# A linear-attention block gated by a spatial-shift MLP: the same instructions in another planned order

## The chip, the cores and the metric

One core of a Trainium2 chip. The time is the device time of one execution in microseconds (us); "before" is the median of three executions. Five engines run instruction queues of their own, each strictly in order: PE (matrix), DVE (vector), ACT (activation), POOL (GpSimd) and SP, which here only issues DMA transfers. They meet through semaphores.

## The reference

With x of 2048 rows and 512 columns, xn its layer norm, and 1376 hidden columns:

```python
phi = lambda t: jnp.where(t > 0, t + 1, jnp.exp(t)) + 1e-6        # 32 heads of 16
num = phi(q) @ (phi(k).T @ v); den = phi(q) . sum(phi(k)) + 1e-6  # per head; q, k, v = xn @ wqkv
s   = (num / den) @ wo
h   = gelu(layernorm(xn) @ w1)          # its four quarters of columns are shifted by
x1  = xn + shifted(h) @ w2              # +1, -1, +2, -2 rows before w2
y   = x1 + gelu(layernorm(x1) @ w3) @ w4
out = x + s * silu(y)
```

All in float32.

## The kernel before

**Tiles.** Rows are taken in 16 tiles of 128 (index i, 0 to 15) and in four blocks of 512 (index b, 0 to 3). Each factor of a product is split into a high and a low part (names ending in h and l), and three matmuls, high by high, low by high and high by low, make one product (`products`, L455). Some products of two-by-two blocks go through `seven` (L749), which makes seven products of 256 columns in three PSUM banks pa, pb and pe; ACT copies finished sums out as p1 and p5 (both shown as p, or pm and the like, in the profile), after which the bank is used again.

**Stages.** First the projections: k (`key`), q (`query`), and `gram`, which adds up k^T xn in four banks g; wq and w1 first have their column means removed (`center`, L546). For wq the four tiles are added on DVE into wqt; for w1 four transfers add them up in the tile w1t, the first by SP and then three accumulating ones by POOL (`gather`); in both cases a matmul (wqm, w1m) makes the column sums from the total. Beside that run the mixer's first product (`mix1`, tiles h and ht), its block forms (`forms`, names hs and ha) and second product (`mix2`, tiles o), then the k-v matrices, then the mixer's two large products (`up_pair`, `down`) with the attention's output (`attend_pair`) between, and the gate and the store (`gate`).

**Scales.** A layer norm takes DVE's bn_stats and bn_aggr (tiles st and mv; L567) and a chain of four small instructions on POOL: add epsilon (w), power of -0.5 (rs, L572), and two small ones for the shift (ns and nm in `scale_x`, L577; nm twice for the second norm). ACT then scales the tile: x for the first norm, y for the second. `scale_u` (L588) makes the per-row factors au of block b in the same way (pu, then power), and `spread_a` (L595) has PE transpose them (bank ab), so that a row of DRAM can be read back by `join_a` (L604) to all partitions as abc.

**Order.** No instruction is issued as the code comes to it. Every one is recorded in a `Plan` (L85) with an engine, a modelled time busy, a modelled latency, its predecessors, and for a transfer its size in MB (`mb`). `deadlines` (L237) gives each PE instruction a nominal time, one after another, and `backward` (L258) gives everything else a due time: that of its successors, less a gap and its own latency, or, for a transfer, less 4.0 us and 4 us per MB. `nudged` (L231) then takes a table of pairs, number of an instruction and quarters of a microsecond, by which that instruction is due sooner (`SOONER`, L1352). `emit` (L264) walks through modelled time: for each engine it lists what could start, keeps those that start within a slack of the earliest, takes the one that is due first, and issues it to that engine's queue. PE may take an instruction out of its recorded order within `window` us of nominal time, and one that opens a new bank within `ahead`. Buffers come from pools with a set number of slots, and SP's and POOL's transfers each go through eight completion slots of their own, so that a transfer waits for the eighth-last of its kind.

The lines that the prediction names: L164 is ACT's activation, L186, L191 and L196 are the two-input, the one-input and the scalar-and-two-input instruction of DVE (or POOL), L145 the matmul, L202 an SP load, L207 an SP store, L220 POOL's accumulating transfer, L569 and L570 the statistics. pqd is the DRAM copy of phi(q): SP stores one part (qr) and POOL adds another (qe). zacc gathers the sums of phi(k) in the same way.

Of the kernel before, what the change touches and what calls it, by code (L numbers as in the profile page):

```python
# [84 lines left out]
class Plan:  # L85
# [82 lines left out]
    def vec(self, eng, out, reads, emit, pair, scalars=0):  # L168
        views = [v for v in reads if isinstance(v, View) and v.n > 4]
        sb = not any(v.tile.psum for v in views + [out])  # L170
        n = max([v.n for v in views] + [out.n])
        if eng == "POOL":
            lat = (.2 if n <= 8 else .15 + n / (435 if pair else 1000))
            return self.add(eng, lat, lat, reads, [out], emit, two=n > 64)
        if pair or not sb:
            lat = .15 + n / 960 + (.06 if scalars else 0)
        else:
            lat = .16 + n / 1920 + (.1 if scalars else 0)
        lat = max(lat, .2)
        self.add(eng, lat - .08, lat, reads, [out], emit, two=sb and n > 8)  # L180
# [77 lines left out]
    def backward(self):  # L258
        for op in reversed(self.ops):
            if op.eng != "PE":  # L260
                for o in op.post:
                    op.due = min(op.due, o.due - self.GAP - (4.0 + op.mb * 4 if op.mb else op.lat))

    def emit(self, first, lead, reserve, window, ahead, table=()):  # L264
        self.deadlines(first)
        self.nudged(table)
        ops = self.ops
        waiting = {op: len(op.pre) for op in ops}
        avail = {e: [] for e in ("PE", "ACT", "DVE", "POOL", "SP")}
        for op in ops:  # L270
            op.ready = 0.0
            if not waiting[op]:
                avail[op.eng].append(op)
        pe = [op for op in ops if op.eng == "PE"]
        head = 0
        free = {e: 0.0 for e in avail}
        slots = {tag: [0.0] * n for tag, n in self.counts.items()}
        port = dma = 0.0
        table = 0
        done = set()  # L280
        slip = 0.0
        left = len(ops)
        while left:
            while head < len(pe) and pe[head] in done:
                head += 1
            front = pe[head] if head < len(pe) else None
            slip = max(0.0, free["PE"] - front.nom) if front else INF
            best = None
            for e, cands in avail.items():
                picks = []  # L290
                low = INF
                for op in cands:
                    s = max(free[e], op.ready)
                    if op.two and s < port:
                        s = port
                    if op.table is not None and op.table != table:
                        s = max(s, free[e] + 1.28)
                    ok = True
                    fresh = [t for t in op.tiles if t.ap is None]
                    for t in fresh:  # L300
                        if t.tag not in slots:
                            continue
                        q = slots[t.tag]
                        need = sum(1 for u in fresh if u.tag == t.tag)
                        if len(q) < need:
                            ok = False
                            break
                        s = max(s, q[need - 1] + self.GAP)
                        if e == "PE":
                            if op is not front and (len(q) < 2 or op.nom - front.nom > ahead):  # L310
                                ok = False
                                break
                        elif t.tag in lead:
                            n = lead[t.tag] * (1.5 if len(q) > reserve[t.tag] else 1)
                            s = max(s, op.due + slip - n - t.early)
                    if not ok:
                        continue
                    if e == "PE" and op.nom - front.nom > window:
                        continue
                    q = s  # L320
                    if op.table is not None and op.table != table and op.due + slip < s:
                        q = s - 1.28
                    picks.append((q, s, op))
                    low = min(low, q)
                if not picks:
                    continue
                slack = .02 if e == "PE" else 0.08
                s, op = min(((s, op) for q, s, op in picks if q <= low + slack), key=lambda x: (x[1].due, x[1].order))
                if best is None or s < best[0]:
                    best = (s, op)  # L330
            if best is None:
                raise RuntimeError("no operation can go: " + str({t: len(q) for t, q in slots.items()}))
            s, op = best
            e = op.eng
            avail[e].remove(op)
            for t in op.tiles:
                if t.ap is None:
                    if t.tag in slots:
                        slots[t.tag].pop(0)
                    t.ap = self.pools[t.tag].tile([t.rows, t.width], t.dtype, tag=t.tag, name=t.name)  # L340
            op.emit()
            op.at = s
            k = self.COLD if e == "PE" and s < self.COLD_TILL else 1.0
            free[e] = s + op.busy * k
            op.end = s + op.lat * k
            if op.mb:
                soft = e == "POOL"
                late = min(.92, 1.03 * max(0.0, dma - s))
                dma = max(dma, s + (.97 if soft else .06)) + op.mb * (4.59 if soft else 3.43)
                op.end = max(dma + (1.89 if soft else 1.29) + late, s + (4.08 if soft else 2.08 if op.loads else 2.2))  # L350
            if op.two:
                port = op.end if e == "POOL" else free[e]
            if op.table is not None:
                table = op.table
            for t in op.tiles:
                t.left -= 1
                t.end = max(t.end, op.end)
                if not t.left and t.tag in slots:
                    slots[t.tag].append(t.end)
            for o in op.post:  # L360
                flow = o.pre[op]
                if o.eng == e == "PE" and not flow:
                    r = 0.0
                elif o.eng == e:
                    r = op.end
                else:
                    r = op.end + self.GAP
                if op.mb:
                    r = max(r, min(r + self.SAFE, o.due + slip - o.lat - self.SAFE))
                o.ready = max(o.ready, r)  # L370
                waiting[o] -= 1
                if not waiting[o]:
                    avail[o.eng].append(o)
            done.add(op)
            left -= 1
# [3 lines left out]
def linear_attn_gated_by_mixer(  # L379
# [43 lines left out]
    pl = Plan(nc, pools, counts, ("acc", "mm"))  # L423
# [147 lines left out]

    def power(out, src, n):  # L572
        nh = nhalf[:, :n]
        pl.add("POOL", .25 + .2 * n, .25 + .2 * n, [src, nh], [out],
               lambda: g.tensor_tensor(out.get(), src.get(), nh.get(), op=ALU.pow))

    def scale_x(lo, n):  # L577

        r = rs1[:, lo:lo + n]
        w = small(f"w{lo}", n).all  # L580
        pl.ts(w, var(mv1, lo, lo + n), EPS, None, ALU.add, eng="POOL")
        power(r, w, n)
        pl.ts(ns1[:, lo:lo + n], r, -1.0, None, ALU.mult, eng="POOL")
        pl.tt(nm1[:, lo:lo + n], means(mv1, lo, lo + n), ns1[:, lo:lo + n], ALU.mult, eng="POOL")
        for i in range(lo, lo + n):
            halves_x(i)
# [660 lines left out]
    for base, s in ((0, 1), (DH - 1, -1)):  # L1247
        v = bmask.all.via(lambda ap: ap.rearrange("p (h d) -> p h d", d=DH))
        pool(.5, [v], v, lambda v=v, base=base, s=s: g.affine_select(
            out=v.get(), in_=v.get(), compare_op=ALU.is_ge, fill=0.0, base=base,  # L1250
# [30 lines left out]
    for b in range(NQ):  # L1281
# [50 lines left out]
        else:  # L1332
# [17 lines left out]
                gate(b * QT + QT - 1, a, o, D // 2, late=True, by_dma=False, whole=o > 0)  # L1350

    SOONER = (  # L1352
        23, 6, 30, 19, 33, 7, 36, 17, 38, 10, 48, 469, 49, 111, 51, 181, 75, 28, 131, 15, 134, 34, 152, -18,
        171, 13, 179, 28, 184, 12, 191, 40, 193, 13, 195, 11, 1656, 8, 2061, 2, 2252, 13, 2382, 10, 2384, 25,
        3174, 3, 3755, 4, 3761, 5, 3874, 15, 4437, 20, 4566, 19,
    )
    pl.emit(first=6.0, lead={"p": 9.0, "w": 20.0, "ab": 10.0}, reserve={"p": 12, "w": 1, "ab": 0}, window=12.0,
            ahead=6.0, table=SOONER)


# [35 lines left out]
```

## Time and profile before

| | |
|---|---|
| median of three runs | 525.2 us (525.14 to 525.43) |
| the profiled execution | 524.78 us |
| its span (first to last instruction) | 523.0 us |
| granted clock of PE | 1.0 |
| first real matmul starts | 5.28 us |
| last matmul starts | 518.08 us |
| DMA moved | 100.13 MB, 191 GB/s in the mean |

The page gives each engine's busy time and the chain of work that ended last; the timeline gives every instruction's start and duration, and in brackets the idle time before it and what ended that. Times in the trace count from the span's start. A matmul's end is modelled and overlaps the next one's start, so PE's stalls are best read from one start to the next.

### The profile page before, as it was taken

To read this page: it belongs to the slowest core of one execution; us is meant where nothing else is said; L and a number is where in the kernel's file an instruction comes from. 1 tells how busy PE (TensorE), PEld (TensorE's weight loads), DVE (VectorE), ACT (ScalarE), POOL (GpSimd) and SP (SyncE) were. 2 spreads that over 40 slices of the span, in tenths; PEclk is the share of its full clock that TensorE was granted. 3 is DMA by queue.
4 is the path that set the end of the run, shared out by engine and by line. 5 is a ranking of instruction groups with operands and counts; after the bars stand their busy time and mean duration, and the time that the engine had idled before them with its cause. 6 is when DMAs were issued, how large, how long until landed. Compare 5 with 4: busy or idle time off the path is not lost.

```text
span 523.0 us, 8865 instructions
## 1 busy us (share of the span) xinstructions
PE 515.3 (99%) x3027; PEld 447.7 (86%) x3027; DVE 373.9 (71%) x743; ACT 317.0 (61%) x649; POOL 110.6 (21%) x207
## 2 busy tenths in 40 slices
PE   8999999999999999999999999999999999999996
PEld 6677888888888888798899889899899898999985
DVE  5977975558465737899996667787666867496835
ACT  4596977397549837859655665546563355543721
POOL 2486322721263032211100022000040000320000
PEclk9999999999999999999999999999999999999999
DMA  8868759672885379989578478949289673894915
GB/s 272 254 158 204 142 97 249 159 173 61 194 237 150 73 154 217 262 234 284 212 248 235 153 217 200 301 120 243 65 186 267 212 201 112 181 291 152 321 45 122
DMA packets 73713, 100.13 MB, mean 191 GB/s; under 512 B 7892, under 2 KB 31716, under 8 KB 73668
## 3 DMA queue, kind: packets, MB, share of 16 engines
q1 hardware_dynamic: 62436, 79.24, 47.2%
q0 software_dynamic: 11088, 20.19, 24.0%
q8 instruction: 24, 0.39, 0.3%
q14 instruction: 21, 0.17, 0.1%
q10 hardware_dynamic: 144, 0.13, 0.1%
HBM read 60.33 MB, written 30.81 MB: 174 GB/s over the span
## 4 chain that ended last, share of the span: by engine, by line
PE 87%; ACT 4%; DVE 3%; DMA 3%; POOL 1%; issue 1%; SPq 0%; ACTq 0%; DVEq 0%; POOLq 0%
PE acc L145 22%; PE pb L145 10%; PE q L145 8%; PE h L145 7%; PE g L145 7%; PE k L145 6%; PE pe L145 5%; PE pbm L145 4%; PE pbs L145 3%; PE pa L145 2%; PE pem L145 2%; PE pes L145 2%; PE s L145 2%; PE a L145 2%; DMA wq_s<-in_wqkv 1%
## 5 line engine op out<-in xcount | busy, mean ns | idle before, releaser
L220 POOL DMA_DIRECT2D xo<-x1d x12 | 10.8, 1158 | 161.9 <-ACT xo L164 107.3
L220 POOL DMA_DIRECT2D th<-in_x x14 | 12.3, 918 | 73.0 <-issue 48.5
L220 POOL DMA_DIRECT2D zacc<-kr x16 | 14.6, 912 | 59.9 <-DVE kr L196 53.2
L164 ACT ACTIVATE p<-pb 128x256 f32<-128x256 f32 x20 | 7.7, 386 | 30.5 <-PE pb L145 30.1
L164 ACT ACTIVATE x<-x,nm,rs 128x512 f32<-128x512 f32 x16 | 12.2, 807 | 19.7 <-POOL nm L186 19.7
L220 POOL DMA_DIRECT2D o<-x x16 | 14.2, 887 | 37.9 <-DVE o L186 29.6
L164 ACT ACTIVATE gf<-gf 128x512 f32<-128x512 f32 (+1 forms) x40 | 20.6, 524 | 0.6
L220 POOL DMA_DIRECT2D pqd<-qe x16 | 16.7, 1042 | 19.2 <-DMA pqd<-qr 9.3
L186 DVE TENSOR_TENSOR gf<-pa,p 128x256 f32<-128x256 f32 x20 | 8.4, 422 | 16.0 <-PE pa L145 9.8
L196 DVE SCALAR_TENSOR_TENSOR kr<-kt,kr 128x512 f32<-128x512 f32 x16 | 11.1, 691 | 11.1 <-ACT kt L164 11.1
L196 DVE SCALAR_TENSOR_TENSOR kt<-wneg,mv,k 128x512 f32<-128x512 f32 x16 | 11.9, 746 | 8.8 <-PE k L145 8.6
L164 ACT ACTIVATE p<-pe 128x256 f32<-128x256 f32 x20 | 7.7, 386 | 15.7 <-PE pe L145 15.7
L164 ACT ACTIVATE th<-xo 128x512 f32<-128x512 f32 (+1 forms) x16 | 9.8, 613 | 11.1 <-DVE xo L186 11.1
L569 DVE BATCH_NORM_STATS2 st<-o 128x6 f32<-128x512 f32 x16 | 10.7, 678 | 4.1 <-DMA o<-x 4.1
L164 ACT ACTIVATE y<-o,nm,rs 128x512 f32<-128x512 f32 x16 | 12.2, 804 | 2.3 <-POOL nm L191 2.3
L164 ACT ACTIVATE qe<-q,ns 128x512 f32<-128x512 f32 x16 | 10.9, 680 | 4.4 <-PE q L145 4.3
L186 DVE TENSOR_TENSOR gf<-u,pe 128x256 f32<-128x256 f32 x20 | 8.3, 413 | 6.2 <-PE pe L145 6.0
L196 DVE SCALAR_TENSOR_TENSOR th<-th,so 128x512 f32<-128x512 f32 (+1 forms) x17 | 11.0, 658 | 1.8 <-ACT th L164 1.1
L164 ACT ACTIVATE kr<-kt,rs 128x512 f32<-128x512 f32 x16 | 11.3, 714 | 1.3 <-DVE kt L196 1.3
L191 POOL TENSOR_SCALAR w<-mv 128x4 f32<-128x4 f32 (+3 forms) x11 | 3.5, 314 | 40.9 <-DVE mv L570 40.6
L154 DVE STREAM_TRANSPOSE y_0z<-y 128x512 f32<-128x512 f32 x8 | 5.7, 712 | 8.8 <-ACT y L164 8.8
L164 ACT ACTIVATE xo<-acc 128x512 f32<-128x512 f32 x12 | 7.2, 598 | 7.6 <-PE acc L145 7.0
(1567 smaller groups left out, 2200.7 us busy)
## 6 DMA issues: line engine op xcount, KB each, us to landing
w_s<-in_w SPq DMA_DIRECT2D x28, 256.0 KB, 5.0
x<-in_x SPq DMA_DIRECT2D x16, 256.0 KB, 4.9
pqd<-qr SPq DMA_DIRECT2D x16, 256.0 KB, 3.3
zacc<-kr POOLq DMA_DIRECT2D x16, 256.0 KB, 4.9
pqd<-qe POOLq DMA_DIRECT2D x16, 256.0 KB, 5.0
o<-x POOLq DMA_DIRECT2D x16, 256.0 KB, 4.0
x1d<-o SPq DMA_DIRECT2D x16, 256.0 KB, 3.9
pq<-pqd SPq DMA_DIRECT2D x16, 256.0 KB, 6.0
```

Of the source, the lines that this page charges most:

```text
L145: lambda: nc.tensor.matmul(out.get(), lhs.get(), rhs.get(), start=start, stop=stop, skip_group_check=more))
L154: self.add("DVE", .60, .67, [src], [out], lambda: self.nc.vector.transpose(out.get(), src.get()))
L164: nc.scalar.activation(out.get(), src.get(), func, scale=get(scale), **kw)
L186: self.vec(eng, out, [a, b], lambda: self.e(eng).tensor_tensor(out.get(), a.get(), b.get(), op=op), True)
L191: lambda: self.e(eng).tensor_scalar(out.get(), a.get(), get(s1), get(s2), **kw), False,
L196: lambda: self.nc.vector.scalar_tensor_tensor(out.get(), a.get(), get(s), b.get(), op0=op0, op1=op1),
L220: lambda: self.nc.gpsimd.dma_start(out.get(), get(src), accum_op=ALU.add), mb=mb)
L569: pl.add("DVE", .62, .69, [xv], [st], lambda: nc.vector.bn_stats(st.get(), xv.get()))
```

## The change

Seven sets of numbers in the planner are altered; no recorded instruction is.

- `vec`: a small POOL instruction (at most 8 elements in a row) is modelled with 0.3 us, before 0.2.
- `power`: POOL's power of n columns is modelled with 0.53 + 0.15 n, before 0.25 + 0.2 n.
- `backward`: a transfer is due 5.0 us and 4 us per MB ahead of its user, before 4.0.
- `emit`: transfers can't start in the model before 0.8, and each waits in the model for the eighth-last transfer of its kind (SP's and ACT's one kind, POOL's the other) to end, plus the gap.
- `emit`: the slack of engines other than PE is 0.15, before 0.08.
- `SOONER`: a new table.
- The last call: `window` 5.0, before 12.0; `ahead` 3.0, before 6.0.

```diff
-            lat = (.2 if n <= 8 else .15 + n / (435 if pair else 1000))
+            lat = (.3 if n <= 8 else .15 + n / (435 if pair else 1000))
...
-                    op.due = min(op.due, o.due - self.GAP - (4.0 + op.mb * 4 if op.mb else op.lat))
+                    op.due = min(op.due, o.due - self.GAP - (5.0 + op.mb * 4 if op.mb else op.lat))
...
-        port = dma = 0.0
+        port, dma = 0.0, 0.8
+        under = [0.0] * 8, [0.0] * 8
...
                     s = max(free[e], op.ready)
+                    if op.mb:
+                        s = max(s, under[e == "POOL"][0] + self.GAP)
...
-                slack = .02 if e == "PE" else 0.08
+                slack = .02 if e == "PE" else 0.15
...
                 op.end = max(dma + (1.89 if soft else 1.29) + late, s + (4.08 if soft else 2.08 if op.loads else 2.2))
+                under[soft].pop(0)
+                under[soft].append(op.end)
...
-        pl.add("POOL", .25 + .2 * n, .25 + .2 * n, [src, nh], [out],
+        pl.add("POOL", .53 + .15 * n, .53 + .15 * n, [src, nh], [out],
...
     SOONER = (
-        23, 6, 30, 19, 33, 7, 36, 17, 38, 10, 48, 469, 49, 111, 51, 181, 75, 28, 131, 15, 134, 34, 152, -18,
-        171, 13, 179, 28, 184, 12, 191, 40, 193, 13, 195, 11, 1656, 8, 2061, 2, 2252, 13, 2382, 10, 2384, 25,
-        3174, 3, 3755, 4, 3761, 5, 3874, 15, 4437, 20, 4566, 19,
+        25, 847, 29, 148, 31, 69, 35, 44, 38, 40, 40, 37, 44, 25, 47, 36, 49, 1824, 50, 192, 52, 513, 54, 53,
+        56, 41, 131, 72, 152, 48, 171, 17, 191, 45, 193, 42, 195, 38, 196, 31, 331, 17, 1342, 6, 1842, 11,
+        4458, 9, 4547, 17, 4548, 7, 4568, 20, 4714, -11,
     )
-    pl.emit(first=6.0, lead={"p": 9.0, "w": 20.0, "ab": 10.0}, reserve={"p": 12, "w": 1, "ab": 0}, window=12.0,
-            ahead=6.0, table=SOONER)
+    pl.emit(first=6.0, lead={"p": 9.0, "w": 20.0, "ab": 10.0}, reserve={"p": 12, "w": 1, "ab": 0}, window=5.0,
+            ahead=3.0, table=SOONER)
```

Four places in the queues where the new order differs, in the words of the instructions' names:

- SP's first loads, from the eighth on. Before: xt0_0, wq_s1, xt0_3, wq_s0, xt0_1, x1, wq_s2, xt0_2, wq_s3, xt0_3, x3, x2, w1t. After: xt0_3, xt0_0, xt0_1, x2, xt0_3, xt0_2, wq_s0 to wq_s3, x1, w1t, x3.
- POOL at block 1. Before: the chain of x4, pu1, au1, then pqd1<-qe1. After: pqd1<-qe1, w4, pu1, au1, then the rest of the chain of x4. The second and third accumulating transfers into w1t come earlier.
- PE: w1m comes ahead of the fourth gram; k0 and k1 begin ahead of ksum.
- ACT in blocks 2 and 3: at block 2, hs33h and the scaled tiles y8, y9, y10 come ahead of ht3_3 and y11; at block 3, y12 and y13 both come ahead of the copy p of the first `seven` of the large products that waits there.

## The prediction

> **What bounds the kernel now.** I read the page's first and fourth part, then the list of what the matrix engine waits for, then the timeline of PE around each gap, then the chain of waits for the longest gap.
>
> ```profile
> span 523.0 us, 8865 instructions
> ...
> PE 515.3 (99%) x3027; PEld 447.7 (86%) x3027; DVE 373.9 (71%) x743; ACT 317.0 (61%) x649; POOL 110.6 (21%) x207
> ...
> PE 87%; ACT 4%; DVE 3%; DMA 3%; POOL 1%; issue 1%; SPq 0%; ACTq 0%; DVEq 0%; POOLq 0%
> ```
>
> PE is busy for 99% of the span. Both kernels issue the same matmuls, so a new order can only take away PE's stalls or add some. PE's list of waits (time, times, longest):
>
> ```profile
> PE pe L145 <- ACT p L164: 0.8, 1, 0.8
> ...
> PE q L145 <- DVE wq_0l L186: 0.2, 1, 0.2
> PE k L145 <- DVE wk_0l L186: 0.2, 1, 0.2
> ```
>
> This list counts idle time after the modelled end of the matmul before, so it shows too little: ends overlap the next start. I therefore go by starts. A matmul of 512 columns follows the one before it by 0.23 us, one of 256 columns by 0.12. PE's timeline (start, duration):
>
> ```profile
> 22.95 0.44 PE L145 MATMUL q<-wq_0h,u_0h 128*128 128x512 f32 x1
> 23.62 0.50 PE L145 MATMUL q<-wq_0l,u_0h 128*128 128x512 f32 x1 [0.23 <-DVE wq_0l L186]
> ...
> 25.38 0.39 PE L145 MATMUL q<-wq_1h,u_1h 128*128 128x512 f32 x1
> 25.85 0.51 PE L145 MATMUL q<-wq_1l,u_1h 128*128 128x512 f32 x1
> 26.19 0.39 PE L145 MATMUL q<-wq_1h,u_1l 128*128 128x512 f32 x1
> ```
>
> From 22.95 to 23.62 is 0.67, so 0.44 too long, and the start after a stall is 0.11 late as well (25.85 to 26.19 is 0.34). Adding up all such excesses that an order could take away gives about 4.5 us: some 2.2 before 31 us, 0.7 at 223 to 225, 1.07 at 255 to 256, 0.27 at 488. This is the most that the change can gain. Everything else is matmuls at their pitch, 5.3 us before the first real one and 4.7 after the last.
>
> **The change part by part.** It alters only the numbers by which the planner puts instructions in order; the instructions stay. I took the new order of each engine's queue and put the durations and landings of the traced execution into it. The terms go against that execution (524.78 us, of which 523.0 is span); the median of the runs, 525.2, is 0.42 more.
>
> *Start, to 31 us: -1.4.* SP now loads the pieces of xt and tile x2 before the four wq tiles and x1. PE begins with k0 and k1 in place of ksum, at about 5.55 where it was 5.28; it waits for wk_0l in both orders and is still 0.2 behind at the ninth matmul. With 256 KB landing every 0.7 us, as the first loads do, wq_s is complete at 14.5, early enough for its column sums at 19. The stall of 0.36 at 12.57 (pitch and restart) goes; the lead is 0.2 at 20 us. DVE now does wq_0l, wq_1l and wq_2l one after another, ahead of kt1 and the fourth wq_s; in before, wq_1l (0.61) stood behind two kt, a wq_s and two mv. So the stalls from 22.9 to 26.2 go: 0.44 + 0.11 + 0.15 + 0.10 + 0.24 + 0.11 = 1.15, and 0.24 at 30.15. That is 1.6. What is late next is k1h, since x1 comes last: its mv at 24.5, four POOL operations (1.5 to 2.5 in this trace), kr1 and k1h give 29.0 to 29.25 against PE's need at 29.0 to 29.3. I charge 0.2 for it. Bounds: 2.2 gained, or 0.3 lost if all stalls stay and only the later start is felt.
>
> *b=1's gate, at 49 us: +0.4.* In before POOL does pu1 and au1 (46.96 to 48.29) and then issues the accumulating transfer pqd1<-qe1. In after this issue, which waits for the store pqd1<-qr1 to land, stands ahead of w4, pu1 and au1, and DVE's four st (0.68 each) stand behind the four w1_s. I get mv at 47.2, then w 0.25, pu 0.19, au 1.05 and gaps: 48.6 to 48.9; PE's transpose ab1, at 50.47 in before, is due at 48.9. If the store lands as late as pqd2's in before (47.52), au1 is ready at 50.2: a stall of 1.3. If early, none. I take 0.4, nearer to the second, since pqd1's store is issued ahead of the w2 loads in both orders.
>
> *205 to 226 us: -0.7.* In before mv of b=2 stands behind ht3_1 on DVE; nm is ready at 215.54, and four y (0.80 each) push everything on ACT back, until p1m ends at 223.68 and PE, which could go at 223.52, goes at 223.73; then p5m in the same way. In after st and mv go first (nm at about 213.5) and ht3_3 stands behind three y instead of two, still some 0.5 earlier. Then p1m would end by 223.3. Gone are 0.21 + 0.11 + 0.29 + 0.11. A second ha223h (0.43) now stands ahead of p1m; without the earlier y it would cost that 0.4, the other bound.
>
> *249 to 257 us: -0.75.* The chain of waits in before (start, length):
>
> ```profile
> 252.07 0.30 DVE mv L570 x4
> ...
> 253.10 1.05 POOL rs L575
> ...
> 254.22 0.69 POOL nm L186
> ...
> 255.32 0.81 ACT y L164
> 256.14 0.28 ACT p L164
> ...
> 256.46 0.98 PE pe L145 x6
> ```
>
> The eviction p (0.36) stood behind a y that waited for POOL's chain, and pe came at 256.46 instead of 255.50. In after q1l and gf copies stand behind st: mv at 250.7, nm at 250.7 + 0.1 + 2.85 = 253.65. But two y now stand ahead of p: 253.9 to 255.45, p ends at 255.8. I work in the times of before, since a lead won earlier moves PE and, through the matmuls that they wait for, the others alike; PE needs p at 255.5. Stall 0.3, so 0.96 + 0.11 - 0.3 = 0.77. Bounds: 1.07, and a loss of 0.4 if mv comes no earlier.
>
> Here a rule speaks against fixed durations for POOL. Rows: ns, a median of 0.24, took 0.85 beside a two-input DVE operation and ended 0.09 after it.
>
> ```profile
> 18.60 0.85 POOL L191 TENSOR_SCALAR ns<-rs 128x1 f32<-128x1 f32 x1
> ```
> ```profile
> 18.68 0.68 DVE L196 SCALAR_TENSOR_TENSOR k0l<-kr,k0h 128x512 fp32r<-128x512 f32 x1
> ```
>
> The nm of 254.22 (0.69) likewise ended at 254.91, with a DVE scalar_tensor_tensor that ran from 254.17 to 254.86. The Trainium skill ("SBUF — State Buffer", "SBUF: two separate sides") has GpSimd and a DVE operation with two SBUF inputs exclude each other for a whole instruction; the trace agrees with these 0.05 to 0.09 us. By it a duration belongs to the neighbours: the four operations take 2.0 when free and 3.0 when three of them meet one, an estimate from the rows 0.24, 0.57, 1.05, 0.69 and 0.41, and this term would run from -1.07 to -0.6 with mv as I have it.
>
> *The rest: 0.* The last 60 instructions on each engine are in the same order, so the tail of 4.7 us stays; 0.27 at 488 may go, and the order in between may bring a few small waits (to +1.0).
>
> Sum: -1.4 + 0.4 - 0.7 - 0.75 = -2.45. So 524.78 - 2.45 = 522.33, and with the 0.42 to the median 522.75, say **522.8 us**.
>
> **Rivals.** A measurement of this kernel tells 0.2%, about 1.05 us, from no change.
>
> *Within 0.2% (0.14).* One of the gains is not got and a new stall is: au1's 1.3 and the gain at 255 or at 223 lost gives -1.4 + 1.3 - 0.7 = -0.8, so 524.4. For it: slack at ab1 is 0 to 0.3 us. Against it: three places would have to go wrong out of four. That the change does nothing (525.2) belongs here; against it stand the moved instructions.
>
> *Slower (0.16).* The three accumulating loads into w1t wait for each other's landing on POOL, and their sum w1m, at 46.73 on PE in before, stands some 40 matmuls earlier in after, at about 39.6. The first gets issued near 16, so three of 8.0 us (as zacc<-kr took from 37.46 to 45.48) land at 40 and cost 0.4. PE's queue stands still behind w1m, one for one. From a landing at 43.1 on, 9.0 us for each, the kernel is slower by over 0.2%; at 43.5 it takes 522.8 + 3.9 = 526.7. For it: in before the third landed at 39.90, seven us ahead of its use, and that cover is given up. Against it: rows of these transfers are 4.0 to 7.1.
> The row: 28.45 to 32.50 with little beside it, 32.79 to 39.90 beside four w2 loads. The Trainium skill ("DMA: Bandwidth & Descriptors", "Queues, rings and completion order") lets each DMA engine take turns between queues, packet by packet. By that rule POOL's lone transfer loses about half its turns however many SP has under way, an estimate of 8.1 at most for each, 40.3 for the three and a stall of 0.7; the 7.1 agrees.
>
> *All stalls go (part of faster).* No new one comes: -2.2 - 0.7 - 1.07 - 0.27, so 521.0.
>
> **How the numbers follow.** Faster 0.70: every found stall has its cover in the new order, and two of the four gains are enough. Same 0.14, slower 0.16. The range runs from 521.0 (all stalls gone) to 526.2, the upper edge of no change; what it leaves out is most of the slower case.
>
> **What the profile will show.** Right: no gap over 0.2 us on PE from 22 to 27, none at 223.5 to 225, one of 0.3 or less near 253 to 255 (the same pe, after the lead), first real matmul at 5.5. Wrong: PE waiting for w1t at w1m, for POOL's au at ab1, for k1h, or for loads in the first 20 us; and p behind two y as late as it was.

## The result: 536.7 us, slower by 2.2%

| | before | after |
|---|---|---|
| median in the comparison (six executions each) | 525.17 us | 536.68 us (535.63 to 537.23) |
| ratio, after to before | | 1.0218, interval 1.0204 to 1.0232 |
| profiled execution, and its span | 524.78, 523.0 us | 536.29, 534.4 us |
| granted clock of PE, mean | 1.0 | 0.988 |

The forecast was 522.8 us, in a range from 521.0 to 526.2. The first and fourth part of the page of after, to be held against the rows of before in the prediction:

```profile
span 534.4 us, 8865 instructions
...
PE 519.2 (97%) x3027; PEld 451.3 (84%) x3027; DVE 373.6 (70%) x743; ACT 318.9 (60%) x649; POOL 112.5 (21%) x207
...
PE 80%; DMA 9%; ACT 4%; DVE 3%; POOL 2%; issue 2%; SPq 0%; DVEq 0%; POOLq 0%
```

The matmuls are the same 3027, yet PE is busy for 3.9 us more: with a mean clock of 0.988, part of its work ran at a lower one. And transfers hold 9% of the chain that ended last, where they held 3%. (Helper lines beyond 570 stand five lines further down than in before, the power at L580; in the experiments they stand up to 16 further.) PE's list of waits in after (time, times, longest):

```profile
PE pbm L145 <- DVE o L186: 5.3, 2, 3.3
PE k L145 <- DVE ht L186: 3.1, 1, 3.1
...
PE g L145 <- ACT k1h L164: 0.8, 1, 0.8
PE pb L145 <- DVE gf L186: 0.2, 1, 0.2
```

The waits of before (pe 0.8, q 0.2, k 0.2) are gone, and four new ones stand in their place. To see where each came I compared the start of the matmul of the same number in both traces. Negative is a lead of after.

| matmul | start in before | after less before | what came ahead of it |
|---|---|---|---|
| 129 | 33.98 | -0.64 | the stalls at 22 to 27 gone; k1h late |
| 209 | 52.70 | -0.40 | w1m and ab1, neither late |
| 289 | 71.26 | +4.28 | **k waits for ht, 61.09 to 64.58** |
| 449 | 99.07 | +8.07 | **pbm waits for o3, 95.89 to 98.30** |
| 729 | 154.69 | +13.10 | **pbm waits for o7, 154.57 to 158.26** |
| 1089 | 226.00 | +12.43 | the stalls at 223 to 225 gone |
| 1369 | 266.45 | +12.00 | the stall of pe gone; pb late by 0.33 |
| the span | 523.0 | +11.4 | |

Each term that the prediction worked out is there, within 0.8 us. The three bold rows, which it did not have, are worth 13.5.

**First stall: a chain on POOL.** POOL's timeline of after (start, duration); rs belongs to x4:

```profile
48.73 0.19 POOL L191 TENSOR_SCALAR pu<-mv 128x4 f32<-128x4 f32 x1
49.01 1.04 POOL L580 TENSOR_TENSOR au<-pu,nhalf 128x4 f32<-128x4 f32 x1
50.03 4.42 POOL L580 TENSOR_TENSOR rs<-w,nhalf 128x1 f32<-128x1 f32 x1
```

A power of one column takes 0.58 elsewhere in this trace. Here it took 4.42, from 50.03 to 54.45. DVE's timeline of the same stretch, its last instruction before and the next after:

```profile
53.35 0.68 DVE L186 TENSOR_TENSOR w_f<-w_s,w_s 128x512 f32<-128x512 f32 x1
58.41 0.69 DVE L196 SCALAR_TENSOR_TENSOR kr<-kt,kr 128x512 f32<-128x512 f32 x1 [4.37 <-ACT kt L164]
```

From 49.14 to 54.03 DVE did eight operations with two SBUF inputs without a gap (`w_1l` to the third `w_f`), which is called a train below. rs could have begun beside the second of them, and ended 0.42 after the last. Then everything behind rs is late: ns, on ACT the scaling of x4 and kt (ACT had been idle for 4.13 us by the row of its wait for ns), and on DVE kr4, which stands in its queue ahead of the ht that frees the bank for PE's k. PE's timeline there:

```profile
61.09 0.39 PE L145 MATMUL h<-u_3h,w_3l 128*128 128x512 f32 x1
64.58 0.79 PE L145 MATMUL k<-wk_0h,u_0h 128*128 128x512 f32 x1 [3.10 <-DVE ht L186]
65.17 0.63 PE L145 MATMUL k<-wk_0l,u_0h 128*128 128x512 f32 x1
65.59 0.63 PE L145 MATMUL k<-wk_0h,u_0l 128*128 128x512 f32 x1
...
67.62 0.39 PE L145 MATMUL k<-wk_2l,u_2h 128*128 128x512 f32 x1
```

From 61.09 to 64.58 is 3.26 longer than the pitch, but that is not all: the next starts lie 0.59, 0.42 and 0.43 apart instead of 0.23, until 67.30. That costs 1.42 more. The table of stretches shows why (start and end, length, then busy time and count for PE, PE's weight loads, DVE, ACT and POOL, then PE's granted clock, 0.50, and what the DMA did):

```profile
64.60:66.00 1.40, 1.40 (x3) 1.14 (x4) 1.40 (x3) 1.38 (x2) 0.50 (x1) 0.50 0.29 51
```

PE was granted half its clock from 64.07 to 67.49, of which 2.9 us lie behind the stall.

**Second and third stall: a buffer that a transfer still reads.** The chain of waits of after, followed back from 98.3 (start, length):

```profile
86.53 4.48 DMA pqd<-qr
...
91.56 6.17 DMA pqd<-qe
...
97.82 0.44 DVE o L186
...
98.30 0.80 PE pbm L145 x2
```

The subtraction o<-pbm,p5m, which frees bank pbm for PE, waits for the transfer pqd<-qe of block 1. The two share no data. They share a buffer: tile o3 of the mixer is handed the buffer from which qe6 is still being added to DRAM, and that transfer had itself waited for the store pqd<-qr to land. The same happens 59 us later with o7 and qe10. DVE's list of waits gives both; in before that list has no such line:

```profile
DVE o L186 <- DMA pqd<-qe: 5.5, 2, 3.4
```

In before it is parts u of later xt tiles that wait for such a transfer (POOL's u_1l for 1.6 us, ACT's u_2h for 2.6), and PE has no stall at either place. Which tile gets a buffer is nobody's choice: a pool hands out what has come free, so every shift in the order of releases deals the buffers anew. The two stalls cost 2.19 and 3.46 against the pitch, and some 1.6 of half clock after each.

### The profile page after: what moved, and what is told of

The parts are those of the page before. It is cut to its first block, busy times and chain, and to the rows that moved or that the text cites. A ratio compares the mean times of both kernels' runs of the same rounds, so it can differ in the third digit from the quotient of the medians.

```text
span 534.4 us, 8865 instructions
## 1 busy us (share of the span) xinstructions
PE 519.2 (97%) x3027; PEld 451.3 (84%) x3027; DVE 373.6 (70%) x743; ACT 318.9 (60%) x649; POOL 112.5 (21%) x207
## 4 chain that ended last, share of the span: by engine, by line
PE 80%; DMA 9%; ACT 4%; DVE 3%; POOL 2%; issue 2%; SPq 0%; DVEq 0%; POOLq 0%
PE acc L145 22%; PE pb L145 11%; PE h L145 6%; PE q L145 6%; PE g L145 5%; PE pe L145 5%; PE k L145 5%; PE pbm L145 4%; PE pbs L145 3%; DMA pqd<-qe 3%; PE pa L145 3%; DMA w1t<-in_w 2%; PE s L145 2%; DMA pqd<-qr 2%; PE pes L145 2%; PE pem L145 2%
## 5 line engine op out<-in xcount | busy, mean ns | idle before, releaser
L164 ACT ACTIVATE th<-xo 128x512 f32<-128x512 f32 (+1 forms) x16 | 9.6, 615 | 13.8 <-DVE xo L186 11.4
L580 POOL TENSOR_TENSOR rs<-w,nhalf 128x4 f32<-128x4 f32 (+3 forms) x11 | 14.2, 1292 | 0.8
L164 ACT ACTIVATE o<-pbm 128x256 f32<-128x256 f32 x8 | 3.1, 385 | 18.4 <-PE pbm L145 18.4
L164 ACT ACTIVATE kr<-kt,rs 128x512 f32<-128x512 f32 x16 | 11.4, 715 | 2.5 <-POOL rs L580 1.4
L164 ACT ACTIVATE kt<-kt,rs 128x512 f32<-128x512 f32 x16 | 11.6, 724 | 0.4
```

What stands on the lines that cost most here:

```text
L164: nc.scalar.activation(out.get(), src.get(), func, scale=get(scale), **kw)
```

## The experiments

In the kernels e1 to e4, e6 and e7 the planner's order is worked out first, as it was, and then single named instructions are put elsewhere in their queues, or single tiles get buffers of a pool that has idle ones at that time. Except in e8 the edits are shown in words, not in code.

**e1: own buffers for qe6 and qe10.**

```diff
-    qe6, qe10: from the pool that o3 and o7 use as well
+    qe6, qe10: from the pool of the wide weight tiles
```

> The changed kernel's order, with the two tiles qe6 and qe10 in buffers of the pool w, which is idle until 200 us, so that o3 and o7 no longer draw a buffer that a transfer still reads. Theory (buffers): of the 11.5 us that the change lost, 3.8 at 96 us and 5.1 at 155 us come from PE waiting for o3 and o7, the stall itself (2.2 and 3.5) and the half clock after it (1.6 each). So 536.7 - 8.9 = 527.8 us, and no gap over 0.3 us on PE at these two places. Rival (transfers): pqd<-qr and pqd<-qe are late by themselves and something else behind them holds PE: then the gaps stay and the time stays at 536 to 537.

528.53 us, ratio to before 1.0092 (1.0059 to 1.0125), 0.7 from what was expected. Both waits of pbm are gone; rs still takes 4.41 and ht is late by 3.26. So the shared buffer is the cause of those two stalls, worth 8.2 us by the medians, and the first stall is another matter. As long as in after, it costs no clock in this profiled execution: three of the five took 528.1 to 528.5 us at a mean clock of 0.996 to 0.999, the other two 531.9 and 532.0 at 0.988 and 0.990.

**e2: the scales in the order of before.**

```diff
 DVE, block 1:
-    st st st st mv mv mv mv
+    st mv st mv st mv st mv
 POOL, block 1:
-    zacc<-kr, u_3, pqd1<-qe1, w, pu1, au1, rs, ns, nm
+    zacc<-kr, w, rs, ns, nm, pu1, au1, u_3, pqd1<-qe1
```

> The changed kernel's order, with nine instructions of POOL and DVE at 45 to 55 us put back as they were before the change: each mv behind its st, and POOL's w4, rs, ns, nm, pu1, au1 ahead of u1_3l and of the transfer pqd1<-qe1. Theory (train): rs of x4 took 4.4 us because DVE ran seven instructions with two SBUF inputs without a break from 49.7 to 54.0; ahead of that train it takes 0.6, x4 and kr4 come some 5 us earlier, ht is not behind them any more, and the stall of 3.3 us at 61 us goes with the half clock after it (1.4): 536.7 - 4.7 = 532.0 us. Rival (ht is late for another reason, such as the broadcast abc0 or the w2 forms on DVE): the stall stays, 536 to 537.

533.15 us (530.50 to 534.53), ratio 1.0151 (1.0119 to 1.0183). rs takes 0.58 and the stall of ht is gone. The two waits of pbm stay, 2.67 and 2.63 longer than the pitch. Only one of them costs clock as well. The stretches right behind the one and the other, columns as above:

```profile
95.00:96.40 1.40, 1.40 (x6) 1.40 (x7) 1.40 (x3) 0.00 (x0) 0.00 (x0) 0.50 1.14 206
154.00:155.40 1.40, 1.40 (x9) 1.31 (x10) 1.40 (x3) 0.39 (x1) 0.00 (x0) 1.00 1.01 183
```

Clock 0.50 and six matmuls behind the first, 1.00 and nine behind the second: equal stalls, and one is 1.5 us dearer.

**e3: both.**

```diff
+    the edits of e1 and of e2
```

> Both edits together, the buffers of qe6 and qe10 and the order of the scale chain of x4. If the three stalls are all that the change lost, they add up: 536.7 - 8.9 - 4.7 = 523.1 us, 2.1 below the kernel before, which is what the gains at the start, at 223 and at 255 us leave in the two traces. If stalls hide one another (one removed lets the next appear), it is above 525.

524.52 us, ratio 0.9997 (0.9981 to 1.0012): none of the three stalls is left, and the kernel is no slower than before. Of the 1.4 that it lacks to what was expected, 0.8 is a k1h that is later still, by 1.75 where it was 0.96 in after:

```profile
PE g L149 <- ACT k1h L168: 1.6, 1, 1.6
```

**e4: rs alone ahead of pu1.** Is it the instruction rs, or the moment, that takes 4.4 us?

```diff
-    w, pu1, au1, rs, ns, nm
+    w, rs, pu1, au1, ns, nm
```

> The changed kernel's order with one instruction moved: POOL does rs of x4 ahead of pu1 and au1 in place of behind them. Theory (train): the long wait belongs to the moment, not to the instruction: rs takes 0.6 and now pu1 or au1 takes over 4 us, until DVE's train ends at 54.0; au1 ends near 55.3 where PE needs it at 50.1, so PE stalls 5 us at ab1, with 1.5 of half clock behind it, and the stall at 61 shrinks: 536.7 + 6.5 - 4.7 = 538.5 us, at least above 537. Rival (power): rs itself is slow, because of its own code or because it comes right behind another power: pu1 and au1 take 1.3 as before, rs is short or not, and the time falls to 532 or stays.

538.09 us from two executions (536.75 and 539.44), ratio 1.0251 (1.0216 to 1.0286). rs took 0.58, and pu1, 0.19 in after, now stayed out:

```profile
49.43 4.69 POOL L195 TENSOR_SCALAR pu<-mv 128x4 f32<-128x4 f32 x1
```

au1 came 5 us late and PE waited at ab1. The long duration goes with the place in the queue, beside DVE's run of two-input operations, and not with the power.

**e5: POOL beside DVE, and PE after gaps, by themselves.**

```diff
+    ten subtractions (or bn_stats, or subtractions from PSUM) back to back on DVE; beside them 0 to 3 small
+    instructions and then powers of 1 or 4 columns on POOL; then bursts of matmuls with growing gaps between
```

> None of the block's computation, only the disputed waits (the output is zeros). First 48 trials: a small DVE result releases a chain on POOL (none to three small instructions, then a power of one column, of four, or of four and then one), while DVE runs nothing, ten subtractions with two SBUF inputs, ten bn_stats (one SBUF input) or ten subtractions with one PSUM and one SBUF input, 512 columns each, without a break. Theory (train): beside two-input instructions a chain takes until the train's end (6 us) in many of the trials; beside the three others it takes its 0.6 to 2.5 us. Rival (one at a time): POOL waits only for the instruction under way, 0.6 at most for each of its own. Rival (power after power): the second of two powers is slow beside nothing too. Then bursts of matmuls with idle gaps between them that grow from 1 to 7 us: if the matmul's pitch doubles for some us behind a gap, the shortest gap that does it lies between 1.0 (no loss in the changed kernel) and 2.2 us (loss), and the loss behind it is 1.4 to 1.7 us whatever the gap.

Beside subtractions with two SBUF inputs the power of one column took 0.88 to 0.93 instead of 0.57 (0.78 right behind another power), that of four 1.34 to 1.39 instead of 1.02, a small one 0.52 to 0.56 instead of 0.19. Beside bn_stats, or a subtraction with one input in PSUM, nothing was added. POOL waited for the subtraction under way and no longer; none stayed out for the ten. So the train theory failed here in its simple form. For PE, the gaps (start to start less the pitch) and what followed them:

| gap, us | 1.28 | 1.82 | 2.27 | 2.74 | 3.21 | 3.66 | 4.58 |
|---|---|---|---|---|---|---|---|
| matmuls at a pitch of 0.43 | 0 | 0 | 7 | 0 | 0 | 8 | 9, from the first on |

A gap between 2.2 and 3.7 us halves the clock for the next matmuls at some moments and not at others. The traces show at which. In the ten traces with the block's matmuls or these bursts (before, after, e1 to e8) the granted clock changes only at points that lie 3.41 us, or a whole multiple of it, apart. Cut at these points, e2 reads as follows at its two equal stalls (start and end, length, PE's busy time and count, granted clock, and what the DMA did):

```profile
91.43:94.84 3.41, 1.05 (x6) 1.00 1.00 248
94.84:98.26 3.42, 3.28 (x11) 0.50 0.65 117
149.46:152.87 3.41, 2.04 (x13) 1.00 1.09 314
152.87:156.28 3.41, 2.31 (x13) 1.00 0.80 145
```

The first stall lies almost whole in one stretch, which leaves PE 1.05 us of work, and the next stretch runs at half clock. The second stall is cut in two, and neither part leaves PE under 2.0. Cut in this way, the ten traces have 20 stretches at full clock in which PE was busy for 1.53 us or less, and half clock followed each of them; in the other 1363 it was busy for 1.66 or more, and half clock followed none. (Busy time is by the modelled ends of the matmuls.)

**e6: e3, and the second accumulating load into w1t behind the scales of x1.**

```diff
 POOL, at 24 us (e3):
-    w1t<-in_w, u_1h, w, rs, ns, nm
+    u_1h, w, rs, ns, nm, w1t<-in_w
```

> The version with both edits, and POOL issues the second accumulating load into w1t behind the scale chain of x1 in place of ahead of it. There POOL stood 8 us in all waiting for the first load to land, with x1's chain behind it, and PE waits 0.6 to 1.8 us for k1h. Theory: that stall goes whole or by most, 524.5 - 1.2 = 523.3 us. Rival: w1t is complete so much later (the second load starts 1.7 us later, the third behind it) that w1m stalls PE instead: 524 to 526.

522.36 us (522.24 to 522.83), ratio 0.9949 (0.9935 to 0.9963): faster than both before and after by more than 0.2%, and 0.4 from the forecast for the change. k1h is in time. Its span, and all that PE still waits for behind its warm-up:

```profile
span 520.4 us, 8869 instructions
```
```profile
PE k L149 <- DVE wk_0h L195: 0.3, 1, 0.3
PE ab L154 <- POOL au L596: 0.2, 1, 0.2
PE pb L149 <- DVE gf L190: 0.2, 1, 0.2
```

**e7: the order of before, with the buffers shared as in after.**

```diff
+    (order of before) qe6 and qe10 share buffers with o3 and o7
```

> The kernel before, its order untouched; the tiles qe6, x7l, o3 and qe10, x11l, o7 lie in the two buffers of the pool w, so that o3 has to wait until the transfer pqd6<-qe6 has read its buffer, and o7 for pqd10<-qe10, as in the changed kernel. Theory (buffers): this alone brings the two stalls at 91 and 146 us into the kernel before, 525.0 + 3.8 + 5.1 = 534 us, somewhat less if the transfers land sooner here (94.3 at the first, where o3 is due at 91.2). Rival (the order of the transfers is what made them late): under 528.

533.48 us, ratio 1.0162 (1.0135 to 1.0189). PE's and DVE's lists:

```profile
PE pbm L149 <- DVE o L190: 4.8, 2, 2.9
```
```profile
DVE o L190 <- DMA pqd<-qe: 5.3, 2, 3.2
```

No instruction stands elsewhere than in before, and the kernel is 8.4 us slower. Compared by the starts of the same matmuls, it falls back by 4.6 at o3 and by 3.7 at o7.

**e8: before with only POOL's two new durations.**

```diff
-            lat = (.2 if n <= 8 else .15 + n / (435 if pair else 1000))
+            lat = (.3 if n <= 8 else .15 + n / (435 if pair else 1000))
...
-        pl.add("POOL", .25 + .2 * n, .25 + .2 * n, [src, nh], [out],
+        pl.add("POOL", .53 + .15 * n, .53 + .15 * n, [src, nh], [out],
```

> The kernel before with one part of the change alone: the planner's two durations for POOL (0.3 for a small instruction, 0.53 + 0.15 n for a power). In the order that follows, x4's chain stays ahead of pu1 and au1 and of the train of subtractions, and qe6's buffer goes to u2_2h, a tile that ACT writes, and not to o3. Theory: the loss hangs on where the order puts two tiles and one chain, not on this part: 523 to 527 us, no gap over 1 us on PE after 30 us but that which ACT may get from u2_2h at 90. Rival: the longer durations alone move POOL's chains so that the time rises to 530 or more.

524.35 us, ratio 0.9992 (0.9982 to 1.0002). This part by itself does nothing that can be told from no change, and brings none of the stalls. Which of the other parts of the change bring them was not tried.

**e9, e10, e11: why did POOL stay out of every boundary?** e5 had not reproduced the 4.4 us. Three more kernels of the same make looked for the condition.

```diff
+    e9:  single instructions of POOL, of several kinds and output types, beside trains of ten
+    e10: single instructions, let go by ACT in steps that cover the whole 0.60 us of a subtraction
+    e11: two instructions, the second right behind the first, the first begun ahead of the train or inside it
```

> None of the block's computation (the output is zeros). 93 trials of one POOL instruction beside ten subtractions of DVE with two SBUF inputs, 512 columns, without a break; a bn_stats of 16 to 496 columns ahead of the train shifts the train's start against POOL's by about 0.017 us from trial to trial, over some 0.5 us of the subtraction's 0.60. POOL's instruction is a power of one column beside float32 outputs, a tensor_scalar of four columns, or a power beside float32r inputs and outputs as the kernel has them. In the trials before, at a distance of 0.17 to 0.22 and 0.32 us from a subtraction's start, POOL got in at that subtraction's end; in the changed kernel, at 0.26 to 0.30, it did not get in until the train ended. Theory (moment): whether POOL gets in hangs on when its request falls within the subtraction; trials near 0.26 to 0.30 take over 4 us, the others under 1.3. Rival (kind): it hangs on float32r, then all or many trials of the last kind are long, whatever the moment. Rival (neither): no trial is long, and what kept POOL out of the train in the kernel is something that only the whole kernel has (transfers, ACT, PE).

> None of the block's computation (the output is zeros). In the sweep before, POOL's small instructions were themselves let in only at the ends of subtractions, so that the one under test always came 0.14 to 0.23 us behind a subtraction's start, and none was long. Here ACT releases it: one or two ACT instructions whose length grows by 12 columns (0.01 us) from trial to trial run beside the train, which ACT's reads don't disturb, so that POOL's request falls anywhere within the 0.60 us of a subtraction. 168 trials, half with a power, half with a tensor_scalar of four columns, beside ten subtractions with a float32r input and output. Theory (moment): requests 0.26 to 0.30 us behind a start (as in the three kernels in which POOL stood 4 us) stay out until the train ends, the others get in at the next end. Rival (neither): none stays out for longer than the subtraction under way, and the cause needs something else that the kernel has.

> The block's computation is left out and zeros are stored; ten two-SBUF-input subtractions stand back to back on VectorE in each trial, behind two operations with one PSUM input, or behind none, and GpSimd gets two instructions directly one behind the other, the first let go at moments from 0.55 us ahead of the train to 1.0 us into it. What is open: in three kernels an instruction of GpSimd that stood directly behind another one, the first begun ahead of the train (rs behind au, pu behind rs), stayed out for the whole train of seven or eight subtractions (4.4 to 4.7 us), while single requests at any moment were let in at the next boundary. If the pair with its first begun ahead of the train is what shuts the second out, seconds of 4 to 6 us stand in the trials whose first starts up to 0.4 us ahead of the train, and none in trials with the first inside it. If it is not, no instruction is longer than its own length (1.0, 0.56, 0.19) and one subtraction (0.6), and the cause of the length of the three stays open.

e9: 93 trials, no instruction beyond 0.99; but the instructions under test all started 0.12 to 0.23 us behind the start of a subtraction, and the three long ones 0.26 to 0.30. So e9 spoke against the kind and left the moment open. e10: 168 trials at 0.08 to 0.57 us, the longest, 1.01, again with a wait for one boundary (the end of one subtraction and the start of the next). The two ends of that sweep, a power of one column let go just ahead of a boundary and just after one (start, duration):

```profile
282.42 0.55 POOL L56 TENSOR_TENSOR rpow<-mpow,epow 128x1 f32<-128x1 f32 x1 [6.22 <-ACT epow L51]
289.31 1.01 POOL L56 TENSOR_TENSOR rpow<-mpow,epow 128x1 f32<-128x1 f32 x1 [6.34 <-ACT epow L51]
```

e11: 264 pairs, the first let go from some 0.8 ahead of the train to 1.67 into it; the longest of all took 1.59, a power of four columns and one subtraction. The block itself speaks against the moment too: nm, 0.27 behind the start of a two-input operation in before and 0.29 in after (58.70), got in at its end and took 0.47 and 0.45. So neither the kind, nor the moment alone, nor standing right behind another instruction keeps POOL out. **That it stayed out for a whole train in after, e1 and e4 is shown; what decides it is open.** No other computing instruction of POOL took 2 us in any trace of this study (the longest are two casts of u_0h in e8, one queued behind the other, 1.99 together), and each of the three ended with the train: 0.42 and 0.41 behind its end for the power, 0.06 for the small one, as if let in there.

## Why the prediction was wrong, point by point

- *Start, -1.4:* -0.64. The stalls from 22.9 to 26.2 went as worked out: after has no gap over 0.1 beyond the pitch there. The term mis-sized is k1h, charged 0.2 and found 0.96, and 1.75 in e1 and e3. POOL's queue was not read for it: x1's w starts at 25.53, behind an issue that stood waiting for a load to land (the bracket is the idle time):

```profile
24.36 0.88 POOL L220 DMA_DIRECT2D w1t<-in_w  x1 [3.49 <-DMA w1t<-in_w]
```

  e6, which moves this issue, shows that it was the cause. (The stalls that the prediction names add up to 4.24 us, not 4.5; its 521.0 is worked out from the 4.24.)
- *ab1, +0.4:* none. au1 ended at 50.05 and ab1 went at 50.10. The issue of pqd1<-qe1 ahead of it did not have to wait: it went at 46.81. The end without a stall came, but by luck: au1 was over 1.1 us later than the 48.6 to 48.9 worked out (0.8 of it by mv, which ended at 47.99), PE reached ab1 1.2 us later than the 48.9, and 0.05 us was to spare.
- *205 to 226 us, -0.7:* 13.10 to 12.43, that is -0.67.
- *249 to 257 us, -0.75:* 12.63 (matmul 1209) to 12.00, that is -0.63. The stall of pe went as a whole, where 0.3 of it was to stay, and one of pb (0.33), which was not in the term, came.
- *The rest, 0 (to +1.0):* **this step failed.** It measured +13.4: 13.5 in three places, less 0.1 in small change. The prediction looked for stalls that go, and for what is late next at the same place. Of the instructions that moved it did not ask what each newly waits for. Two such waits were in the queues of after to be read: o3's and o7's on POOL's transfers (by e1 and e7, 8.2 and 8.4 us), and ht's place behind kr4, and so behind the chain of x4, with rs now beside DVE's w2 forms (e2: 3.5 less than after; e3: 4.0 less than e1).
- *The rule on the shared port* was given as 2.0 to 3.0 us for four instructions, that is at most one subtraction for each. That is what e5, e10 and e11 show. The 4.4 us of one rs could not be had from it. The Trainium skill ("SBUF — State Buffer", "SBUF: two separate sides") lets whichever of the two starts first keep the port for its whole instruction. The trace agrees as far as POOL's wait for a subtraction goes; in the other direction it differs, since the subtractions went on at a pitch of 0.60 to 0.64 while a power of 1.02 us ran (e11).
- *The clock* was in no term. Each of the three stalls cost 1.4 to 1.6 us more by half clock, 4.7 of the 13.5. The Trainium skill ("TensorE: Matmul & The Clock Gate", "Part 1: The HAM clock gate (the "warmup" mystery)") has the clock halved after an idle window of some 3.4 us that runs free of the kernel. The traces agree with its length and that it runs free: the clock changes at points 3.41 us apart, and e2's equal stalls differ by where these cut them. They differ from it in that the window need not be idle: half clock came behind one with 1.53 us of work in it (e7, 150.43 to 153.85).
- *Rival, slower by w1m:* did not come. The three loads into w1t took 4.6 to 7.5 us each, the last landed at 36.87, and w1m, which PE reached at 40.7, had no stall. The kernel is slower by mechanisms that were on no list.
- *Rival, within 0.2%:* its stall at ab1 did not come either. *All stalls go, 521.0:* e6 comes nearest, at 522.36.

So the forecast was near for the places it looked at, but for k1h: with the buffers and the scales put right the new order takes 524.5 us, and 522.4 only with the load moved as well, where 522.8 was forecast for it as it stood.

## What to carry to other kernels

When a planner moves hundreds of instructions, don't price only the stalls that you know: list every wait in the new queues that the old ones didn't have, waits for buffers among them, and for each the engine's queue behind it. A tile that shares a pool with the source of a slow transfer can stall the fastest engine without sharing any data, and a pool deals its buffers anew with every change of order; give the sources of queued transfers buffers of their own. A stall of the matrix engine of over 2 us may cost some 1.5 us more in clock.

## What the runs showed of the hardware

- **POOL and DVE.** Beside DVE instructions with two SBUF inputs, an instruction of POOL waits for the one under way (0.22 to 0.37 more in e5, at most 0.57 in e11) and then runs beside the next, which starts 0.04 late at most. In three of the block's kernels it was kept out until the end of a train, for seven or eight operations, and took 4.4 to 4.7 us; 525 trials in e9, e10 and e11 did not show why.
- **PE's clock.** The granted clock changed only at points 3.41 us, or a multiple, apart; half clock followed a stretch of that length at full clock whenever PE was busy in it for 1.53 us or less, and never with 1.66 or more (1383 such stretches in ten traces). So where these points cut a stall decides: one of 2.05 us cost clock (e7) and one of 3.26 did not (e1). None up to 1.82 did, and with 4.58 (e5) the very first matmul was slow. The price was 7 to 9 matmuls of 512 columns at 0.43 instead of 0.23.
- **Chained transfers.** An accumulating transfer behind a store to the same place took 6.17 us, beside four loads of x, on top of the store's 4.48 (after, 86.53 to 97.73), so that its source was free only 11.2 us after the store went out.
